# Issue order at the start of a one-core attention and two-FFN kernel, and scores one product later

## The chip, the cores and the metric

One core of a Trainium2 chip runs the whole program. The metric is the device time of one execution in microseconds (us), the median of several. TensorE (PE) does matrix products and transposes; ScalarE (ACT), VectorE (DVE) and GpSimd (POOL) work element by element; SyncE (SP) issues most transfers (DMA). Each engine works through its own queue of instructions in order, and semaphores hold an instruction until what it reads has been written and what it overwrites has been read. PSUM is the memory that TensorE writes; SBUF holds everything else.

## The reference

```python
B, H, S, Ns, D = 8, 8, 512, 32, 64
sc  = x @ state.T / sqrt(D);  a  = exp(sc  - max);  a  /= a.sum(-1)  + 1e-9;  xread = a  @ state
sc2 = state @ x.T / sqrt(D);  a2 = exp(sc2 - max);  a2 /= a2.sum(-1) + 1e-9;  sread = a2 @ x
y = concatenate([xread, sread], axis=2)      # per batch 544 tokens, 512 wide after the reshape
y = (silu(y @ w_gate) * (y @ w_val)) @ w_out                 # 512 -> 1536 -> 512
h = y @ w_in                                                 # 512 -> 2048
out = (maximum(h, 0) + alpha * minimum(h, 0)) @ w_out2       # 2048 -> 512
```

The weights arrive as float64, x and state as float32.

## The kernel before

**Products in parts.** Each operand of a large product is split into a high part, rounded for the fast fp32 mode of TensorE, and a low part (the rest), and each product is three passes: high by high, high by low, low by high (`PASSES`, line 19). A split is one ACT copy (`acopy`, line 77) and one DVE subtraction (`sub_lo`, line 83). The second pass needs the low part.

**Weights.** A `Unit` (line 243) turns 1 MB of float64 words into float32: a load (line 255), two passes on ACT (lines 264 and 265), and for each half two bit operations on DVE (lines 271 and 273) and an addition on POOL (line 278 into the tile `wr` of gate and value weights, line 281 otherwise). `Stream.step` (line 306) issues one half step: the ACT passes of one unit, the bits of the unit before it, the use of the one before that. `wr` number 0 needs units 0 and 1, number 1 units 2 and 3.

**Attention.** Of each of the 8 batches ("blocks"), heads go in two groups, u (g=0) and v (g=1). `xt` transposes x (blocks 0 and 1 on TensorE, line 151, with an ACT copy out of PSUM; the others on DVE); `scores` (line 159) are products with the state. For a first softmax, over the state's 32 entries, `first_cols`, `first_max`, `first_exp`, `first_scale` and `first_parts` work (the subtraction of the maximum at line 170 and the scaling at line 181 are on POOL; the result is transposed into `at` and split into `a`); for a second one, over the tokens, `second_max`, `second_exp`, `second_scale` (transposes, line 209) and `second_read` (line 219). The product of `a` with the state is folded into the first FFN: `state_times_w` (line 403) multiplies the state with `wr`, the result is split into `sw`, and gate and value are products of `sw` with `a` (`Block.product`, line 432).

**Stages.** First blocks 0 and 1 together, while weights still arrive: the list `order` (line 640) has 12 steps of gate, value, gate, value for one block and one weight tile; after the second gate of each step stands the `state_times_w` of the next. Their hidden values wait in SBUF. Then the projections of blocks 0 and 1 (`split`, `project`, line 462), with block 2's attention in between. Then blocks 2 to 7 one after the other in `ffn1` (line 473): for f = 0..11 a gate product, slot (f, 0), a value product, the split of the hidden values into `h`, slot (f, 1), the projection of the hidden values of f - 1, slot (f, 2). The slots carry the attention of the next block, `state_times_w` and conversions of the second FFN's weights (`stream2.step`, `one_later`; the tiles `sc` and `sp`). Last the second FFN (lines 769 and 823).

**What sets the order.** TensorE's instructions stand in the order in which the program calls them (`manual_schedule`, line 493). The other engines' queues are ordered by a scheduler that works with priorities by place in the program and with estimates; `tc.issue_after(x)` keeps what is inside behind x. PSUM has eight banks: acc0 to acc3, g, v and two `aux` in turn; an `aux` bank comes free when the last reader of it, often the DVE subtraction of an `sw` split, is done.

Of the kernel before, what the change touches and what calls it, by code (L numbers as in the profile page):

```python
# [8 lines left out]
F32 = mybir.dt.float32  # L9
# [3 lines left out]
AF = mybir.ActivationFunctionType  # L13
# [12 lines left out]
def attention_and_two_ffns(ctx: ExitStack, tc: tile.TileContext, x, state, w_gate, w_val,  # L26
# [60 lines left out]
    nc.vector.memset(warm, 0.0)  # L87
    nc.scalar.activation(warm, warm, AF.Exp)
    ident = const.tile([P, P], F32, tag="ident", name="ident")
# [11 lines left out]

    stt, xq, xn, wraw, wo1, sw, a1, srs = {}, {}, {}, {}, {}, {}, {}, []

    def load_state(b, eng=nc.sync):
        t = sm.tile([P, H, Ns], F32, tag="st", name=name("st"), bufs=1)
        for hp in range(2):
            for e in range(2):
                q = 64 * hp + 32 * e
                eng.dma_start(t[q:q + 32], state[b, :, :, 32 * e:32 * e + 32].rearrange("h n d -> n h d"))
        for hp in range(2):  # L110
            q = slice(64 * hp, 64 * hp + 64)
            for jj in range(2):
                h = 4 * jj + 2 * hp
                nc.vector.transpose(out=bd[b % 2][q, jj, :, Ns * hp:Ns * hp + Ns], in_=t[q, h:h + 2])
        stt[b] = sm.tile([P, H, Ns], F32, tag="stt", name=name("stt"), bufs=2)
        nc.vector.transpose(out=stt[b].rearrange("p h n -> p (h n)"), in_=t.rearrange("p h n -> p (h n)"))
# [11 lines left out]
    def load_xn(b, g):  # L128
        src = x[b].rearrange("(h g) (p c) d -> g p h c d", g=NG, c=SC)[g]
        if b < XT:  # L130
            t = t4([P, SC, 4, D], F32, "xn")
            for h in range(4):
                (nc.scalar if b == 0 and g and h % 2 else nc.sync).dma_start(t[:, :, h], src[:, h])
        else:
# [5 lines left out]
    class Attention:  # L140
# [42 lines left out]
        def first_parts(self, lo=True):  # L183
            b, g = self.b, self.g
            self.at = t2([P, S], F32, "at")
            nc.vector.transpose(out=self.at, in_=self.s1.rearrange("p t n -> p (t n)"))
# [56 lines left out]
    class Unit:  # L243
# [23 lines left out]
        def bits(self, i):  # L267
# [4 lines left out]
                                    op1=ALU.logical_shift_left)  # L272
            nc.vector.scalar_tensor_tensor(out=m, in0=hi, scalar=-0x80000000, in1=t, op0=ALU.bitwise_and,  # L273
                                           op1=ALU.bitwise_or)
            if self.place:
# [143 lines left out]
    class Block:  # L419
# [27 lines left out]
        def value(self, f):  # L447
            nc.vector.tensor_tensor(out=self.p[f], in0=self.p[f], in1=self.product(f, 1, "v"), op=ALU.mult)  # L448

# [43 lines left out]
    with tc.manual_schedule(engines={mybir.EngineType.PE}):  # L493
        load_state(0, nc.scalar)
        for g in range(NG):
            load_xn(0, g)
        stream1.load(2)
        for g in range(NG):
            load_xn(1, g)
        load_state(1)  # L500
        stream1.load(4)
        nc.sync.dma_start(alpha_sb, alpha.rearrange("(k p) -> p k", p=P))
        u, v = att[0, 0], att[0, 1]
        w, z = units1[0], units1[1]
# [16 lines left out]
        w.bits(0)  # L521
        v.second_max()
        v.first_exp()
# [5 lines left out]
        z.bits(0)  # L529
        z.bits(1)  # L530
        q.product()
        u.second_exp()
        p.product()
        q.parts()
        v.second_exp()
        v.first_parts()
        p.parts()
        stream1.skip(2)
        stream1.step(4)
# [17 lines left out]
        def ffn1_slots(b):  # L557
# [20 lines left out]
            if b + 1 < B:  # L578
# [5 lines left out]
                for f, th in attention(nb, (2, 3, 5, 6, 6), 4):  # L584
                    put(f, 0, th)
                put(NF1 - 2, 2, lambda: state_times_w(nb, 0))
# [39 lines left out]
        def raise_all():  # L626
            with tc.issue_after(gates[1].ins):
                for t in (u, v):
                    t.first_exp()
                    t.second_exp()  # L630

        extra = {0: [[lambda: u.xt(0), lambda: u.xt(1), u.scores, u.first_cols],
                     [lambda: v.xt(0), lambda: v.xt(1), u.first_max, u.second_max],
                     [v.scores, v.first_cols, v.first_max, v.second_max], [raise_all, u.first_scale]],
                 1: [[v.first_scale], [u.first_parts], [v.first_parts], []],
# [4 lines left out]
        order = [(0, 0), (0, 1), (1, 0), (1, 1)] + [(b, j) for j in range(2, NJ1) for b in range(XT)]  # L640
        gates = []
        for n, (b, j) in enumerate(order):
            for i in range(4):
                f = 2 * j + i // 2
                if i % 2:
                    blocks[b].value(f)
                elif n == 1 and i == 0:
                    with tc.issue_after(v.raised2.ins):
                        gates.append(blocks[b].gate(f))
                else:  # L650
                    gates.append(blocks[b].gate(f))
                for th in extra.get(n, ((),) * 4)[i]:
                    th()
                if i % 2:
                    stream1.step()
                if i == 2 and n + 1 < len(order):
                    nb, nj = order[n + 1]
                    stream1.until(2 * nj + 1, 1)
                    state_times_w(nb, nj)
        stream1.until(2 * NJ1 + EARLY - 1, 1)  # L660
# [16 lines left out]
        for b in range(XT):  # L677
            for f in range(NF1):
                with tc.issue_after(gates[-3 if f < 2 and not b else -1].ins):
                    blocks[b].split(f)  # L680
                if b == 0:
                    stream1.until(2 * NJ1 + f // 2, 2)
                if f or b:
# [264 lines left out]
```

## Time and profile before

| what | value |
|---|---|
| median of 3 runs | 1445.13 us (1442.11 to 1447.69) |
| the profiled execution's own time | 1446.67 us |
| its span in the profile | 1444.9 us |
| mean granted TensorE clock | 0.986 |
| TensorE busy | 1396.0 us, 97% |
| VectorE, ScalarE, GpSimd busy | 955.5, 516.0, 172.7 us |

The span runs from the first to the last instruction that the profiler recorded; 1.8 us of the execution's own time lie around it. TensorE works almost without a break, so the profile is read by where TensorE stands idle and which engine releases it, and by the clock that it was granted.

### The profile page before, as it was taken

How to read it: one execution, taken by the hardware profiler on the slowest of the kernel's cores; microseconds unless marked ns; L12 is line 12 of the kernel's file. 1: busy time of each engine (PE TensorE's matmuls, PEld its weight loads, DVE VectorE, ACT ScalarE, POOL GpSimd, SP SyncE). 2: the span in 40 equal slices, each digit the busy share in tenths (PEclk: the TensorE clock that was granted, in tenths of full speed). 3: DMA queues.
4: the chain of work that ended last, by engine and by line, in shares of the span. 5: the costliest groups of instructions: out<-in, count | busy, mean ns of one | idle time of the engine just before them, and what ended most of it. 6: DMA issues, size and time to landing. Idle time of an engine off the chain costs nothing.

```text
span 1444.9 us, 18973 instructions
## 1 busy us (share of the span) xinstructions
PE 1396.0 (97%) x7352; PEld 1094.0 (76%) x7352; DVE 955.5 (66%) x1606; ACT 516.0 (36%) x822; POOL 172.7 (12%) x150
## 2 busy tenths in 40 slices
PE   3899999999999999999999999999999999999997
PEld 1566877766767776777988888888888888888886
DVE  5686746778687776434746668676867668666653
ACT  4766335555464644434522112211222112211111
POOL 3351211324232332000000000000000000000000
PEclk6899999999999999999999999999999999999999
DMA  9443314364556443010546324742375324733465
GB/s 255 160 126 93 89 32 121 119 204 161 186 160 202 138 142 121 27 34 11 202 182 218 114 77 182 264 170 91 132 254 221 114 88 182 260 118 124 146 218 205
DMA packets 141586, 214.64 MB, mean 149 GB/s; under 512 B 78008, under 2 KB 85176, under 8 KB 136376
## 3 DMA queue, kind: packets, MB, share of 16 engines
q1 hardware_dynamic: 139352, 213.03, 44.0%
q8 instruction: 58, 0.95, 0.3%
q10 hardware_dynamic: 2144, 0.39, 0.1%
q14 instruction: 32, 0.26, 0.1%
HBM read 169.88 MB, written 43.52 MB: 148 GB/s over the span
## 4 chain that ended last, share of the span: by engine, by line
PE 85%; DVE 5%; ACT 4%; DMA 3%; issue 2%; POOL 0%; ACTq 0%; SPq 0%; DVEq 0%; POOLq 0%
PE acc L462 16%; PE acc L823 14%; PE aux L823 12%; PE v L769 9%; PE v L432 9%; PE g L432 8%; PE aux L769 6%; PE g L769 6%; PE aux L403 3%; DMA xn<-in_x_dram 2%; PE v L873 1%; PE g L873 1%; ACT h L77 1%; ACT raw L264 1%; DVE sw L83 1%
## 5 line engine op out<-in xcount | busy, mean ns | idle before, releaser
L462 PE MATMUL acc<-h,wp 128*128 128x512 f32 (+1 forms) x1296 | 294.9, 378 | 0.0
L462 PEld LDWEIGHTS acc<-h,wp 128*128 128x128 f32 x1296 | 233.4, 188 | 48.7 <-issue 2.5
L77 ACT ACTIVATE h<-m 128x512 fp32r<-128x512 f32 (+1 forms) x144 | 87.6, 609 | 448.3 <-DVE m L754 448.3
L823 PE MATMUL acc<-wo,h 128*128 128x512 f32 x864 | 219.9, 390 | 2.0 <-ACT h L77 1.7
L823 PE MATMUL aux<-wo,h 128*128 128x512 f32 x768 | 194.9, 389 | 0.0
L823 PEld LDWEIGHTS acc<-wo,h 128*128 128x128 f32 x864 | 161.1, 188 | 35.5 <-ACT h L77 2.1
L775 DVE TENSOR_TENSOR u<-v,p 128x512 f32<-128x512 f32 x96 | 66.2, 690 | 168.4 <-PE v L769 167.8
L823 PEld LDWEIGHTS aux<-wo,h 128*128 128x128 f32 x768 | 144.2, 188 | 29.9
L432 PE MATMUL g<-a,sw 128*128 128x512 f32 x576 | 154.2, 403 | 4.6 <-ACT sw L77 3.4
L432 PE MATMUL v<-a,sw 128*128 128x512 f32 x576 | 153.9, 403 | 1.2 <-DVE m L273 0.9
L432 PEld LDWEIGHTS g<-a,sw 128*128 128x128 f32 x576 | 105.6, 190 | 59.1 <-issue 20.1
L769 PE MATMUL v<-x,w 128*128 128x512 f32 x576 | 146.2, 389 | 0.0
L432 PEld LDWEIGHTS v<-a,sw 128*128 128x128 f32 x576 | 105.1, 189 | 42.8 <-issue 14.8
L769 PEld LDWEIGHTS v<-x,w 128*128 128x128 f32 x576 | 108.1, 188 | 22.4
L83 DVE TENSOR_TENSOR h<-m,h 128x512 fp32r<-128x512 f32 (+1 forms) x144 | 94.7, 658 | 16.1 <-ACT h L77 12.8
L448 DVE TENSOR_TENSOR s<-s,v 128x512 f32<-128x512 f32 (+1 forms) x84 | 54.1, 644 | 76.2 <-PE v L432 66.1
L769 PE MATMUL g<-x,w 128*128 128x512 f32 x384 | 97.6, 389 | 0.0
L769 PE MATMUL aux<-x,w 128*128 128x512 f32 x384 | 97.4, 389 | 0.0
L83 DVE TENSOR_TENSOR sw<-aux,sw 128x512 fp32r<-128x512 f32 x96 | 62.6, 681 | 52.3 <-ACT sw L77 52.1
L77 ACT ACTIVATE h<-s 128x512 fp32r<-128x512 f32 (+1 forms) x84 | 50.3, 599 | 98.1 <-DVE s L448 97.5
L281 POOL TENSOR_TENSOR m<-m,raw 128x512 int32<-128x512 int32 x44 | 62.8, 1429 | 183.6 <-DVE m L273 80.8
L769 PEld LDWEIGHTS aux<-x,w 128*128 128x128 f32 x384 | 72.1, 188 | 14.9
(120 smaller groups left out, 1606.9 us busy)
## 6 DMA issues: line engine op xcount, KB each, us to landing
w<-w2d SPq DMA_DIRECT2D x64, 896.0 KB, 6.2
wo<-wo2d SPq DMA_DIRECT2D x40, 1024.0 KB, 6.7
w2d<-sp SPq DMA_DIRECT2D x32, 512.0 KB, 2.7
raw<-in_moe_w_out_dram SPq DMA_DIRECT2D x14, 1024.0 KB, 5.3
out_dram<-o SPq DMA_DIRECT2D x34, 256.0 KB, 2.4
x2d<-xo SPq DMA_DIRECT2D x32, 256.0 KB, 2.5
raw<-in_moe_w_in_dram SPq DMA_DIRECT2D x8, 1024.0 KB, 8.1
wo2d<-sp SPq DMA_DIRECT2D x16, 512.0 KB, 3.6
```

The lines of the kernel that those rows point to most:

```text
L77: return nc.scalar.activation(o, i, AF.Copy)
L83: (eng or nc.vector).tensor_tensor(out=o, in0=src, in1=hi.bitcast(F32), op=ALU.subtract)
L264: nc.scalar.activation(hi.bitcast(F32), hi.bitcast(F32), AF.Copy, scale=REBIAS)
L281: nc.gpsimd.tensor_tensor(out=m, in0=m, in1=lo, op=ALU.add)
L403: nc.tensor.matmul(self.o[Ns * c:Ns * (c + 1), :], stt[b][q, 2 * c + g, :], wraw[j][q, c].rearrange("p k f -> p (k f)"), start=True, stop= ...
L432: nc.tensor.matmul(o[:, :self.n], self.lhs(f, k, a, which), self.rhs(k, c), start=(i == 0), stop=(i == last))
L448: nc.vector.tensor_tensor(out=self.p[f], in0=self.p[f], in1=self.product(f, 1, "v"), op=ALU.mult)
L462: nc.tensor.matmul(self.acc[e][:, :self.n], wo1[f // 2][:, f % 2, a, e * P:(e + 1) * P], t[:, c, :self.n], start=(f == 0 and i == 0), stop ...
L769: nc.tensor.matmul(o, w[a][:, q, c], x[k][:, q, e], start=start and n == 0, stop=stop and n == 5, skip_group_check=True)
L775: nc.vector.tensor_tensor(out=o, in0=x0, in1=x1, op=ALU.add)
L823: nc.tensor.matmul(o, h[:, c, a, u * P:(u + 1) * P], wos2[t][:, f, q], start=start and f == 0 and i == 0, stop=stop and f == 1 and i == 2)
L873: nc.tensor.matmul(o, w[a][:, k % 2, c], x[k // 2][:, k % 2, e, :NS], start=n == 0, stop=n == 11)
```

## The change

- Of block 0's x, group v, the parts h = 2 and 3 are now issued by ACT (before h = 1 and 3), and ACT issues them behind the first of its four state transfers and ahead of the other three. The first activation of the program (`warm`, with the load of its table) comes behind the last of them.
- Block 1's state is loaded from SP behind the raw weights of units 2 and 3 and the 8 KB of alpha; before it stood ahead of them.
- `at` of block 0 lies in the PSUM banks g and v.
- The 16 transposes of block 1's x stand ahead of the first `state_times_w` on TensorE; before they stood behind the first and second product. `second_max` and `second_exp` of v come later.
- In the two-block stage the steps of the weight stream are issued ahead of the step's attention work and are held behind the gate before last; the splits and the last conversions are held behind values too.
- In blocks 2 to 6 the scores of the next block (with what follows them in that stage) move from slot (f, 0) to slot (f, 1) for f = 3 and 7, which puts the value product ahead of them: ten places.

```diff
     nc.vector.memset(warm, 0.0)
-    nc.scalar.activation(warm, warm, AF.Exp)
...
     stt, xq, xn, wraw, wo1, sw, a1, srs = {}, {}, {}, {}, {}, {}, {}, []
+    issued = []
...
                 q = 64 * hp + 32 * e
-                eng.dma_start(t[q:q + 32], state[b, :, :, 32 * e:32 * e + 32].rearrange("h n d -> n h d"))
+                issued.append(eng.dma_start(
+                    t[q:q + 32], state[b, :, :, 32 * e:32 * e + 32].rearrange("h n d -> n h d")))
...
         if b < XT:
             t = t4([P, SC, 4, D], F32, "xn")
             for h in range(4):
-                (nc.scalar if b == 0 and g and h % 2 else nc.sync).dma_start(t[:, :, h], src[:, h])
+                (nc.scalar if b == 0 and g and h > 1 else nc.sync).dma_start(t[:, :, h], src[:, h])
         else:
...
         def first_parts(self, lo=True):
             b, g = self.b, self.g
-            self.at = t2([P, S], F32, "at")
+            self.at = psum([P, S], "v" if g else "g") if b == 0 else t2([P, S], F32, "at")
             nc.vector.transpose(out=self.at, in_=self.s1.rearrange("p t n -> p (t n)"))
...
-            nc.vector.scalar_tensor_tensor(out=m, in0=hi, scalar=-0x80000000, in1=t, op0=ALU.bitwise_and,
-                                           op1=ALU.bitwise_or)
+            self.made = nc.vector.scalar_tensor_tensor(
+                out=m, in0=hi, scalar=-0x80000000, in1=t, op0=ALU.bitwise_and, op1=ALU.bitwise_or)
...
         def value(self, f):
-            nc.vector.tensor_tensor(out=self.p[f], in0=self.p[f], in1=self.product(f, 1, "v"), op=ALU.mult)
+            return nc.vector.tensor_tensor(out=self.p[f], in0=self.p[f], in1=self.product(f, 1, "v"),
+                                           op=ALU.mult)
...
     with tc.manual_schedule(engines={mybir.EngineType.PE}):
-        load_state(0, nc.scalar)
         for g in range(NG):
             load_xn(0, g)
+        load_state(0, nc.scalar)
         stream1.load(2)
         for g in range(NG):
             load_xn(1, g)
-        load_state(1)
         stream1.load(4)
         nc.sync.dma_start(alpha_sb, alpha.rearrange("(k p) -> p k", p=P))
+        with tc.issue_after(issued[-1].ins):
+            nc.scalar.activation(warm, warm, AF.Exp)
         u, v = att[0, 0], att[0, 1]
         w, z = units1[0], units1[1]
         p, q = StateTimesW(0, 0, 0), StateTimesW(0, 0, 1)
             w.act()
         v.first_max()
         w.bits(0)
-        v.second_max()
...
         w.bits(1)
         with tc.issue_after(u.raised1.ins):
         u.first_parts()
         z.bits(0)
         z.bits(1)
+        for t in (att[1, 0], att[1, 1]):
+            t.xt(0)
+            t.xt(1)
         q.product()
         u.second_exp()
         p.product()
         q.parts()
-        v.second_exp()
         v.first_parts()
         p.parts()
+        v.second_max()
+        v.second_exp()
+        load_state(1)
         stream1.skip(2)
...
                 for f, th in attention(nb, (2, 3, 5, 6, 6), 4):
-                    put(f, 0, th)
...
-        extra = {0: [[lambda: u.xt(0), lambda: u.xt(1), u.scores, u.first_cols],
-                     [lambda: v.xt(0), lambda: v.xt(1), u.first_max, u.second_max],
-                     [v.scores, v.first_cols, v.first_max, v.second_max], [raise_all, u.first_scale]],
+        def columns(t):
+            t.scores()
+            with tc.issue_after(units1[3].made.ins):
+                t.first_cols()
+
+        extra = {0: [[lambda: columns(u)], [lambda: columns(v), u.first_max, u.second_max],
+                     [v.first_max, v.second_max], [raise_all, u.first_scale]],
...
-        gates = []
...
                 if i % 2:
-                    blocks[b].value(f)
+                    values.append(blocks[b].value(f))
...
                     gates.append(blocks[b].gate(f))
+                with tc.issue_after(gates[max(0, len(gates) - 2)].ins):
+                    if n == i == 0:
+                        stream1.until(3, 1)
+                    if i % 2:
+                        stream1.step()
+                    if i == 2 and n + 1 < len(order):
+                        stream1.until(2 * order[n + 1][1] + 1, 1)
                 for th in extra.get(n, ((),) * 4)[i]:
                     th()
-                if i % 2:
-                    stream1.step()
                 if i == 2 and n + 1 < len(order):
-                    nb, nj = order[n + 1]
-                    stream1.until(2 * nj + 1, 1)
-                    state_times_w(nb, nj)
+                    state_times_w(*order[n + 1])
...
-                with tc.issue_after(gates[-3 if f < 2 and not b else -1].ins):
+                k = -3 if f < 2 and not b else -1
+                with tc.issue_after(gates[k].ins), tc.issue_after(values[k].ins):
                     blocks[b].split(f)
                 if b == 0:
-                    stream1.until(2 * NJ1 + f // 2, 2)
+                    with tc.issue_after(values[-1].ins):
+                        stream1.until(2 * NJ1 + f // 2, 2)
```

POOL at the start of the program, from u's scaling on; `s_18`/`s_16` are u's softmax tile, `s_25`/`s_23` v's, `s_65`/`s_74` block 1's, `wr` weight tiles, `raw_137`/`raw_136` unit 0, `raw_140`/`raw_139` unit 1, `raw_164`/`raw_152` and `raw_167`/`raw_155` units 2 and 3. Before:

```order
L181 TENSOR_TENSOR s_18_188<-s_18_188,r_27_216 128x512
L181 TENSOR_TENSOR s_25_210<-s_25_210,r_35_243 128x512
L278 TENSOR_TENSOR wr_230<-m_29_226,raw_137 128x2x256
L278 TENSOR_TENSOR wr_230<-m_33_236,raw_137 128x2x256
L278 TENSOR_TENSOR wr_230<-m_38_253,raw_140 128x2x256
L278 TENSOR_TENSOR wr_230<-m_40_258,raw_140 128x2x256
L278 TENSOR_TENSOR wr_305<-m_53_301,raw_164 128x2x256
L278 TENSOR_TENSOR wr_305<-m_56_307,raw_164 128x2x256
L170 TENSOR_TENSOR s_65_338<-s_65_338,m_71_362 128x512
L278 TENSOR_TENSOR wr_305<-m_74_373,raw_167 128x2x256
```

and now:

```order
L182 TENSOR_TENSOR s_16_177<-s_16_177,r_25_205 128x512
L279 TENSOR_TENSOR wr_219<-m_27_215,raw_136 128x2x256
L279 TENSOR_TENSOR wr_219<-m_30_222,raw_136 128x2x256
L182 TENSOR_TENSOR s_23_199<-s_23_199,r_32_229 128x512
L279 TENSOR_TENSOR wr_219<-m_35_239,raw_139 128x2x256
L279 TENSOR_TENSOR wr_219<-m_37_244,raw_139 128x2x256
L279 TENSOR_TENSOR wr_333<-m_61_329,raw_152 128x2x256
L279 TENSOR_TENSOR wr_333<-m_64_335,raw_152 128x2x256
L279 TENSOR_TENSOR wr_333<-m_69_354,raw_155 128x2x256
L279 TENSOR_TENSOR wr_333<-m_71_359,raw_155 128x2x256
L171 TENSOR_TENSOR s_74_367<-s_74_367,m_82_393 128x512
```

The first two conversions moved ahead of v's scaling, and those of units 2 and 3 ahead of the subtractions of block 1 (line 170 before, 171 now).

ACT near the end of the two-block stage, ahead of the split of the `sw` that belongs to the last weight tile and block 0 (`sw_1100` before, `sw_1112` now). Before:

```order
L445 ACTIVATE p_1070<-g_1092 128x512
L265 ACTIVATE raw_1061<-raw_1061 128x1024
L77 ACTIVATE sw_1100<-aux_1101 128x512
L77 ACTIVATE sw_1100<-aux_1106 128x512
L77 ACTIVATE wp_1132<-m_214_1065 128x512
```

and now:

```order
L446 ACTIVATE p_1075<-g_1104 128x512
L265 ACTIVATE raw_968<-raw_968 128x1024
L266 ACTIVATE raw_968<-raw_968 128x1024
L265 ACTIVATE raw_1092<-raw_1092 128x1024
L77 ACTIVATE sw_1112<-aux_1113 128x512
L77 ACTIVATE sw_1112<-aux_1118 128x512
L266 ACTIVATE raw_1092<-raw_1092 128x1024
```

Where one conversion pass stood between the second gate's activation and the split, three stand now.

DVE in block 3, from the value of f = 4 on; `h_2845` is the hidden tile of that f, `v_2837` and `v_2911` the value products of f = 4 and 5, `sw_2868` the next step's split, `e2t_2909` the copy of the transposes. Before (the seven rows that follow are alike in both):

```order
L448 TENSOR_TENSOR s_2816<-s_2816,v_2837 128x512
L83 TENSOR_TENSOR h_2845<-s_2816,h_2845 128x512
L83 TENSOR_TENSOR sw_2868<-aux_2869,sw_2868 128x512
L83 TENSOR_TENSOR sw_2868<-aux_2874,sw_2868 128x512
L271 TENSOR_SCALAR m_527_2852<-raw_2479 128x512
```

and now:

```order
L449 TENSOR_TENSOR s_2816<-s_2816,v_2837 128x512
L83 TENSOR_TENSOR sw_2868<-aux_2869,sw_2868 128x512
L83 TENSOR_TENSOR sw_2868<-aux_2874,sw_2868 128x512
L272 TENSOR_SCALAR m_527_2852<-raw_2479 128x512
L352 TENSOR_TENSOR sc_2883<-m_456_2483,m_465_2539 128x128
L274 SCALAR_TENSOR_TENSOR m_527_2852<-raw_2479,m_527_2852 128x512
L352 TENSOR_TENSOR sc_2883<-sc_2883,m_456_2483 128x128
L352 TENSOR_TENSOR sc_2883<-m_456_2483 128x128
L352 TENSOR_TENSOR sc_2883<-m_465_2539,sc_2883 128x128
L80 COPY e2t_2909<-aux_2904 128x512
L449 TENSOR_TENSOR s_2888<-s_2888,v_2911 128x512
L83 TENSOR_TENSOR h_2845<-s_2816,h_2845 128x512
```

The subtraction that makes the low part of `h_2845` moved from the second row to the last, behind the value of f = 5. On TensorE the projection of `h_2845` stands right behind `v_2911` in both. The same is found in blocks 4 and 5 at the same f (`h_3615`, `h_4385`) and at no other of the ten places.

## Rows read from the trace of the kernel before

**Rows 1.** The page, part 1: busy time and share of the span, TensorE.
```profile
PE 1396.0 (97%) x7352; PEld 1094.0 (76%) x7352; DVE 955.5 (66%) x1606; ACT 516.0 (36%) x822; POOL 172.7 (12%) x150
```

**Rows 2.** Windows: busy us by engine, then granted clock, DMA share, GB/s.
```profile
0.00:20.00 20.00, 7.97 (x24) 3.87 (x24) 5.65 (x17) 7.43 (x10) 1.75 (x7) 0.79 0.86 220
20.00:36.00 16.00, 4.43 (x17) 0.90 (x18) 15.67 (x35) 9.06 (x14) 10.56 (x9) 0.50 0.94 298
36.00:60.00 24.00, 19.88 (x80) 11.80 (x79) 14.59 (x30) 18.43 (x26) 9.27 (x9) 0.79 0.68 242
60.00:140.00 80.00, 76.79 (x555) 50.66 (x554) 60.14 (x109) 52.62 (x77) 26.60 (x21) 1.00 0.29 87
```

**Rows 3.** Waits of TensorE, 0 to 250 us: total, times, longest.
```profile
PE aux L403 <- POOL wr L278: 14.8, 3, 10.3
PE aux L151 <- DMA xn<-in_x_dram: 9.3, 2, 5.1
PE g L432 <- ACT sw L77: 3.4, 3, 2.2
...
PE v L432 <- DVE m L273: 0.9, 1, 0.9
PE g L432 <- DVE sw L83: 0.8, 2, 0.5
PE g L432 <- ACT p L445: 0.4, 1, 0.4
```

**Rows 4.** Timeline of TensorE, first 57 us: start, length, engine, line; idle before.
```profile
7.27 1.95 PE L159 MATMUL acc<-xt,bd 128*64 128x512 f32 x4
13.43 1.94 PE L151 MATMUL aux<-ident,xn 128*128 128x128 f32 x8 [4.20 <-DMA xn<-in_x_dram]
...
31.31 1.95 PE L403 MATMUL aux<-wr,stt 64*32 64x512 f32 x12 [1.04 <-POOL wr L278]
35.44 3.07 PE L432 MATMUL g<-a,sw 128*128 128x512 f32 x6 [2.18 <-ACT sw L77]
38.31 1.39 PE L151 MATMUL aux<-ident,xn 128*128 128x128 f32 x8
...
42.99 1.04 PE L151 MATMUL aux<-ident,xn 128*128 128x128 f32 x8
...
50.80 1.95 PE L403 MATMUL aux<-wr,stt 64*32 64x512 f32 x12 [3.40 <-POOL wr L278]
52.67 2.93 PE L432 MATMUL v<-a,sw 128*128 128x512 f32 x6
```

**Rows 5.** Timeline of GpSimd, first 52 us.
```profile
25.77 5.48 POOL L278 TENSOR_TENSOR wr<-m,raw 128x512 int32<-128x512 int32 x4
...
49.46 1.28 POOL L278 TENSOR_TENSOR wr<-m,raw 128x512 int32<-128x512 int32 x1
```

**Rows 6.** Timeline of TensorE near the end of the two-block stage.
```profile
132.25 0.73 PE L432 MATMUL g<-a,sw 128*128 128x512 f32 x2 [0.69 <-ACT sw L77]
```

**Rows 7.** Waits of TensorE, 160 us to the end.
```profile
PE aux L159 <- DVE sw L83: 6.5, 7, 1.0
```

**Rows 8.** Timeline of TensorE, 302 to 326 us, in block 3.
```profile
308.07 1.08 PE L159 MATMUL aux<-xt,bd 128*64 128x512 f32 x4 [0.97 <-DVE sw L83]
...
321.87 1.64 PE L432 MATMUL v<-a,sw 128*128 128x512 f32 x6
323.35 2.89 PE L462 MATMUL acc<-h,wp 128*128 128x512 f32 x12
```

**Rows 9.** Timeline of VectorE, the same stretch.
```profile
319.07 0.69 DVE L83 TENSOR_TENSOR h<-s,h 128x512 fp32r<-128x512 f32 x1 [0.86 <-ACT h L77]
320.62 0.69 DVE L83 TENSOR_TENSOR sw<-aux,sw 128x512 fp32r<-128x512 f32 x1 [0.86 <-ACT sw L77]
...
325.60 0.68 DVE L80 COPY e2t<-aux 128x512 f32<-128x512 f32 x1
```

**Rows 10.** Timeline of ScalarE, the same stretch: one conversion pass.
```profile
320.48 1.14 ACT L264 ACTIVATE raw<-raw 128x1024 f32<-128x1024 f32 x1
```

More of the change, by code (lines that the diff above doesn't have):

```diff
@@ L584, in ffn1_slots @@
                 for f, th in attention(nb, (2, 3, 5, 6, 6), 4):
-                    put(f, 0, th)
+                    put(f, 1 if f in (3, 7) else 0, th)
                 put(NF1 - 2, 2, lambda: state_times_w(nb, 0))
@@ L640, in attention_and_two_ffns @@
         order = [(0, 0), (0, 1), (1, 0), (1, 1)] + [(b, j) for j in range(2, NJ1) for b in range(XT)]
-        gates = []
+        gates, values = [], []
         for n, (b, j) in enumerate(order):
```

## The prediction

> **What bounds the kernel now.** I read the page's busy times first: TensorE is busy 97% [rows 1], so an edit can only win where TensorE stands idle or runs at half clock, and it loses wherever it makes TensorE wait. The windows show where that is: 7.97 of the first 20 us and 4.43 of the next 16 are busy, at a granted clock of 0.79 and 0.50; from 36 to 60 us 19.88 of 24 at 0.79; from 60 to 140 us 76.79 of 80 at full clock [rows 2]. TensorE's waits name the releasers: 14.8 us for POOL's conversions into `wr` (three times), 9.3 us for x (twice), and 3.4 + 0.9 + 0.8 + 0.4 = 5.5 us before gate and value products [rows 3]. After 160 us one wait matters: 6.5 us, seven times, before scores, released by the DVE subtraction that frees their `aux` bank [rows 7]. The timeline then gives each place.
>
> **The start, step by step.** In the timeline u's scores begin at 7.27, v's transposes only at 13.43, after 4.20 us of waiting for x; the first state products end at 33.26 (31.31 + 1.95), held by a train of four conversions, 25.77 to 31.25; the first gate product follows at 35.44, 4.2 us after the train [rows 4, 5].
>
> ACT now issues v's two parts of x ahead of three state transfers. That is 256 KB in front of the state, at the 220 GB/s of the first 20 us [rows 2] an estimated 1.2 us for u's scores: they end near 7.27 + 1.2 + 1.95 = 10.4, and v's transposes start there, 3.0 us sooner. (Bounds: nothing sooner, if the bytes in front keep x as late as now; 4.2 us at most, the wait itself.)
>
> POOL's first two conversions now pass v's scaling. Their bits are made by DVE before 24 us already, so POOL no longer stands idle ahead of its train; with v's operations 3.0 us sooner and four conversions of 5.48 / 4 = 1.37 us, I take the train's end at 26.2, 5.0 us sooner. Behind it the same 4.2 us of state products and splits, and 0.9 us for ACT copies of block 1's transposes, which now stand in ACT's queue there: first gate product 26.2 + 4.2 + 0.9 = 31.3, **4.1 us gained** (bounds 0 and 5.0).
>
> Behind it three things leave TensorE's path. The 16 transposes of block 1 (1.39 + 1.04 us [rows 4]) move into the wait for the train: **2.4**. The wait for the next `wr` (3.40 before 50.80 [rows 4]): the last conversion ended at 49.46 + 1.28 = 50.74 [rows 5], because block 1's subtractions, which wait for scores, stood ahead of it on POOL; now four stand in a row behind the first train, 26.2 + 4 x 1.37 = 31.7 at the soonest, and with the ACT passes and bits that they need near 37. The fourth product needs them at about 40, so the **3.4** goes. What is late next is the split of that step's `sw`, whose length is the same in both. The `at` of block 0 in PSUM, the later state of block 1 and v's later second maximum I cost at nothing: block 1's scores stand behind the first product, and v's second exponential is wanted by transposes two steps later. If that cover is gone, the scores are as late as the state, about a microsecond. Sum by here: 4.1 + 2.4 + 3.4 = 9.9.
>
> The clock: after the 3.40 us wait twelve state matmuls took 1.95 us and the value product 2.93 [rows 4], a granted half clock; the same value product takes 1.64 at full clock [rows 8]. [...] From the rows one value product at half clock costs 2.93 - 1.64 = 1.3 us; I count none, and let 2 us either way go into the range.
>
> **Later in that stage it loses.** ACT's order puts three conversion passes ahead of the split of the last `sw` of block 0, and two passes, two `h` copies and a weight copy ahead of block 1's. A pass is 1.14 us [rows 10]. Behind the last gate's activation (0.6) come three passes (3.4) and the copy of the split (0.6): 4.6 us, against 1.1 of state products and 1.5 of value product on TensorE, so it waits 2.0. For the other: 0.6 + 2.3 + 1.2 + 0.6 + 0.6 = 5.3 against 2.6, so 2.7. Now 0.69 + 0.51 is waited at such a place (the 0.69 is in [rows 6]; the 0.51 is the longer of the two waits for a subtraction, 0.5, in [rows 3]). **Loss 4.7 - 1.2 = 3.5** (bounds 0, if the passes slip into idle time of ACT, and 6). The first stage as a whole: 9.9 - 3.5 = 6.4 gained.
>
> **Later blocks.** Scores now follow the value product (some 1.4 us from start to next start: 321.87 to 323.35 [rows 8]); the wait they had was never above 1.0 [rows 7], so all of the **6.5 us** goes. But at f = 3 of blocks 3, 4 and 5 the order on DVE moves the subtraction of the hidden tile behind the value of the next f. In the trace that subtraction ran at 319.07 [rows 9], four microseconds before its projection at 323.35 [rows 8]. Now DVE first does the two `sw` subtractions (the first at 320.62), bits and sums, the copy that starts at 325.60 [rows 9], the value and then the subtraction. ACT's conversion passes no longer stand between the two copies of `sw`, so I let this run start 0.6 us and end 1.5 us sooner: copy at 324.1, value 324.7, low part ready at 325.9. The value product ends near 322.4, a microsecond sooner than before, and the projection's first pass takes 0.2: it stands from 322.7 to 325.9, **3.2 us**. The transposes ahead wait 0.5 for their `aux` bank. Three places: **11.1 us lost** (bounds: 3.6, if only value and subtraction of 0.6 each follow the value product; 15, if DVE ends its run no sooner than now). Later blocks: 11.1 - 6.5 = 4.6 lost.
>
> **Sum.** -6.4 + 4.6 = -1.8 on the profiled execution's 1446.67 us, which lies 1.5 above the median; on the median of 1445.13 that is **1443.3 us**. 0.5% is 7.2 us, about what a measurement of this kernel can tell from no change.
>
> **Rivals.**
> 1. *The hidden tiles are not late.* The DVE run ends so much sooner that the lower bound holds: 3.6 lost for 6.5 gained. With the start's 6.4 that is -9.3, 1435.8; without the stalls near the end of the first stage 3.5 more, 1432.3. For it: ACT had idle time before the scores. Against: DVE's run between 320.62 and 325.60 is almost gapless [rows 9].
> 2. *x is no sooner.* The DMA engines are 0.86 and 0.94 busy in the first 36 us [rows 2], and the raw weights land as late as the bytes ahead of them. Then the train of conversions does not move; the transposes' 2.4 and the 3.4 stay, 3.5 are lost again, and 4.6 later: +2.3, 1447.4. [...]
> 3. *Conversions ahead of splits in every step (slower).* The steps of the weight stream are now issued ahead of the attention work in all 12 steps of the first stage. If ACT does as at the last two places in all eleven `sw` splits behind the first, at 2.0 us each, that is 22, of which 4.7 are in my sum: -1.8 + 17 = +15, 1460. It is slower than before from about 0.2 us more per split on. For it: the two places seen. Against: waits on splits in this stage are small now, 3.4 + 0.8 of which 2.18 is the first product's [rows 3, 4], and ACT is busy 52.62 of 80 us between 60 and 140 [rows 2].
>
> **How the numbers follow.** Forecast 0.48, rival 1 0.25, rival 2 0.12, rival 3 0.15. The forecast's own range, from its bounds, is 1436 to 1450: a twelfth of it is faster by over 7.2 us, a twentieth slower. Rival 1 is nearly all faster, rival 2 the same, two thirds of rival 3 slower by over 7.2 us, the rest the same. Faster 0.04 + 0.24 = 0.28, slower 0.02 + 0.10 = 0.12, same 0.60. The range 1432 to 1450 leaves out the far side of rival 3 and little else.
>
> **What would show it.** v's transposes near 10.4 us with no long wait for x; the first gate product near 31 us; no wait of 3 us before the second `wr`; waits of about 2 us at the last two `sw` splits; projections begin near 133 instead of 139.87; no waits before scores; three waits of about 3 us, released by the DVE subtraction of `h`, in blocks 3, 4 and 5. The prediction is wrong if the projections of blocks 3 to 5 don't wait, or if many small waits on `sw` appear between 60 and 130 us.

## The result, and the profile after

| | median us | lowest to highest | runs |
|---|---|---|---|
| before | 1444.16 | 1442.11 to 1447.69 | 4 |
| changed | 1465.07 | 1463.95 to 1469.50 | 4 |

The ratio is 1.0148, 95% interval 1.0118 to 1.0178: 20.9 us slower, where 1.8 us faster was forecast and the range ended at 1450. The profiled execution took 1465.55 us with a span of 1463.8 us; its mean granted clock is 0.980 (0.986 before), and TensorE was busy 1411.7 us instead of 1396.0 with the same 7352 matmuls. One execution of scores_back below, of 1570.36 us at a mean granted clock of 0.842 where the nine others had 0.988 to 0.993, is a slow one and is left out of its ratio.

The windows of the changed kernel (columns as in [rows 2]: length, busy us of PE, PEld, DVE, ACT, POOL, then the granted clock, DMA share, GB/s):

```profile
20.00:36.00 16.00, 11.17 (x44) 5.22 (x44) 15.16 (x37) 13.20 (x21) 9.93 (x8) 0.60 0.92 287
36.00:60.00 24.00, 20.48 (x166) 12.91 (x166) 21.45 (x44) 18.45 (x29) 12.36 (x11) 0.93 0.77 278
...
120.00:140.00 20.00, 16.68 (x69) 10.88 (x68) 14.20 (x24) 11.27 (x20) 3.91 (x3) 0.83 0.52 85
...
300.00:400.00 100.00, 94.72 (x526) 67.33 (x524) 70.26 (x129) 52.12 (x85) 30.75 (x26) 0.95 0.53 168
400.00:500.00 100.00, 90.72 (x515) 64.50 (x513) 69.12 (x128) 53.61 (x87) 28.59 (x24) 0.97 0.51 154
500.00:600.00 100.00, 97.95 (x581) 70.43 (x582) 69.63 (x124) 47.03 (x82) 29.20 (x25) 0.98 0.38 123
```

TensorE is better off at the start (11.17 us busy of 16, against 4.43; a clock of 0.93 from 36 to 60 us, against 0.79). But from 120 to 140 us (0.83) and in the three windows from 300 to 600 us (0.95, 0.97, 0.98) the clock is below the 1.00 that all four had before, and idle time grows. The middle one of the three windows of 300 to 600 us, before:

```profile
400.00:500.00 100.00, 97.27 (x591) 69.25 (x584) 77.61 (x140) 54.34 (x91) 31.66 (x27) 1.00 0.52 161
```

The waits of TensorE, 0 to 250 us, answer to [rows 3]:

```profile
PE aux L152 <- DMA xn<-in_x_dram: 7.8, 3, 5.2
PE g L433 <- ACT sw L77: 6.4, 4, 2.2
PE g L433 <- DVE sw L83: 3.2, 3, 1.6
...
PE aux L404 <- POOL wr L279: 2.0, 1, 2.0
```

The wait for `wr` shrank from 14.8 to 2.0 us, those on splits of `sw` grew from 3.4 + 0.8 to 6.4 + 3.2. From 160 us on, against the one row of [rows 7]:

```profile
PE acc L464 <- DVE h L83: 8.6, 3, 2.9
PE aux L210 <- DVE sw L83: 8.0, 6, 2.7
```

The 6.5 us before scores are gone, and 16.6 us stand in their place: three waits for the low part of `h`, six for the `aux` bank of the transposes. The timeline of TensorE shows the first stage's start and end (start, length, engine, line, operation; idle before and releaser):

```profile
11.18 1.69 PE L152 MATMUL aux<-ident,xn 128*128 128x128 f32 x8
...
24.65 3.23 PE L404 MATMUL aux<-wr,stt 64*32 64x512 f32 x16 [2.04 <-POOL wr L279]
30.03 2.93 PE L433 MATMUL g<-a,sw 128*128 128x512 f32 x6 [2.15 <-ACT sw L77]
...
43.42 2.07 PE L433 MATMUL g<-a,sw 128*128 128x512 f32 x4 [1.41 <-DVE sw L83]
...
53.58 1.20 PE L433 MATMUL g<-a,sw 128*128 128x512 f32 x4 [1.61 <-DVE sw L83]
...
117.61 1.92 PE L433 MATMUL g<-a,sw 128*128 128x512 f32 x6 [1.62 <-ACT sw L77]
...
121.76 1.63 PE L433 MATMUL g<-a,sw 128*128 128x512 f32 x6 [0.84 <-DVE m L274]
...
128.17 2.98 PE L433 MATMUL g<-a,sw 128*128 128x512 f32 x6 [2.16 <-ACT sw L77]
131.46 2.93 PE L433 MATMUL v<-a,sw 128*128 128x512 f32 x6 [0.32 <-DVE m L274]
134.19 2.10 PE L433 MATMUL g<-a,sw 128*128 128x512 f32 x6
...
137.49 12.86 PE L464 MATMUL acc<-h,wp 128*128 128x512 f32 x56
```

The first gate product is at 30.03 ([rows 4]: 35.44). Where 3.40 us were waited for the second `wr` before, three waits on splits stand now, 0.51 + 1.41 + 1.61 = 3.5 us between 41 and 54 us (0.55 + 0.28 at such places before). Then 1.62 + 0.84 + 2.16 + 0.32 us of waits near the end, and behind the wait of 2.16 products of 2.98, 2.93 and 2.10 us: the granted clock is 0.58 from 128.0 to 131.0 us and 0.50 from there to 135.2. From 60 to 115 us, at 1.00, such a product takes 1.5 to 1.8. Projections begin at 137.49, where 139.87 stood in the trace of before. In block 3, the place of [rows 8]:

```profile
318.55 0.75 PE L210 MATMUL aux<-ident,e 128*128 128x128 f32 x4 [0.49 <-DVE sw L83]
319.06 1.64 PE L433 MATMUL v<-a,sw 128*128 128x512 f32 x6
320.53 0.39 PE L464 MATMUL acc<-h,wp 128*128 128x512 f32 x1
323.78 5.06 PE L464 MATMUL acc<-h,wp 128*128 128x512 f32 x11 [2.86 <-DVE h L83]
328.64 2.13 PE L433 MATMUL g<-a,sw 128*128 128x512 f32 x6
```

and VectorE there ([rows 9]):

```profile
321.85 0.68 DVE L80 COPY e2t<-aux 128x512 f32<-128x512 f32 x1
322.45 0.67 DVE L449 TENSOR_TENSOR s<-s,v 128x512 f32<-128x512 f32 x1
323.04 1.47 DVE L83 TENSOR_TENSOR h<-s,h 128x512 fp32r<-128x512 f32 x2
```

The copy, the value and the two subtractions run without a gap; the projection's second pass waits 2.86 us for the first of these subtractions, and the eleven matmuls behind the wait take 5.06 us, the gate product 2.13: the granted clock is 0.51 from 323.8 to 330.0 us (twelve took 2.89 before, at 1.00 from 321.8 to 326.0). At f = 9 of blocks 3, 4 and 5 the transposes wait 1.93, 2.70 and 1.94 us. One row of each wait's place and the product behind it, blocks 3 and 5:

```profile
353.62 1.12 PE L210 MATMUL aux<-ident,e 128*128 128x128 f32 x4 [1.93 <-DVE sw L83]
354.39 2.91 PE L433 MATMUL v<-a,sw 128*128 128x512 f32 x6
```

```profile
528.71 0.75 PE L210 MATMUL aux<-ident,e 128*128 128x128 f32 x4 [1.94 <-DVE sw L83]
529.21 1.64 PE L433 MATMUL v<-a,sw 128*128 128x512 f32 x6
```

Behind nearly the same wait the value product takes 2.91 us once, at a granted clock of 0.50 (354.4 to 357.1 us), and 1.64 once, at 1.00 (529.2 to 530.7). What makes the transposes wait there begins on ScalarE, here in block 4:

```profile
429.97 1.14 ACT L265 ACTIVATE raw<-raw 128x1024 f32<-128x1024 f32 x1 [1.30 <-DMA raw<-in_moe_w_out_dram]
431.01 1.11 ACT L266 ACTIVATE raw<-raw 128x1024 int32<-128x1024 uint32 x1
432.14 1.28 ACT L202 ACT_TABLE_LOAD   x1
...
436.05 0.60 ACT L446 ACTIVATE s<-g 128x512 f32<-128x512 f32 x1
438.66 0.63 ACT L77 ACTIVATE h<-s 128x512 fp32r<-128x512 f32 x1 [2.02 <-DVE s L449]
439.20 1.07 ACT L77 ACTIVATE sw<-aux 128x512 fp32r<-128x512 f32 x2
```

Two conversion passes are ahead of the table load for the exponentials now; that load begins 5.5 us behind the scores (at 426.62), where it began 3.1 us behind them before (TensorE's row and ScalarE's, block 4 before):

```profile
416.49 1.08 PE L159 MATMUL aux<-xt,bd 128*64 128x512 f32 x4 [0.87 <-DVE sw L83]
...
419.62 1.28 ACT L201 ACT_TABLE_LOAD   x1 [3.14 <-issue]
```

So the activation of f = 8 comes at 436.05, 4.0 us after its gate product ended (430.49 + 1.52), the value and the `h` copy follow, and the split of `sw`, whose subtraction frees the `aux` bank, is pushed to 439.20. VectorE adds to it: when that activation ends, at 436.65, the last of four sums and a row sum stand ahead of the value on VectorE, which starts 1.3 us later (VectorE's row, then TensorE's):

```profile
437.95 0.67 DVE L449 TENSOR_TENSOR s<-s,v 128x512 f32<-128x512 f32 x1
...
441.39 0.75 PE L210 MATMUL aux<-ident,e 128*128 128x128 f32 x4 [2.70 <-DVE sw L83]
```

### The profile page after: what moved, and what is told of

Read it like the earlier page. It is cut to its first block, busy times and chain, and to the rows that moved or that the text cites. A ratio compares the mean times of both kernels' runs of the same rounds, so it can differ in the third digit from the quotient of the medians.

```text
span 1463.8 us, 19000 instructions
## 1 busy us (share of the span) xinstructions
PE 1411.7 (96%) x7352; PEld 1102.7 (75%) x7352; DVE 950.2 (65%) x1606; ACT 517.0 (35%) x822; POOL 175.1 (12%) x150
## 4 chain that ended last, share of the span: by engine, by line
PE 87%; DVE 5%; ACT 3%; DMA 2%; issue 2%; POOL 0%; SPq 0%; ACTq 0%; DVEq 0%; POOLq 0%
PE acc L464 17%; PE acc L839 13%; PE aux L839 12%; PE g L433 9%; PE v L433 9%; PE v L785 9%; PE aux L785 6%; PE g L785 6%; PE aux L404 3%; DMA raw<-in_moe_w_out_dram 1%; ACT raw L265 1%; PE v L889 1%; PE g L889 1%; DVE sw L83 1%; DVE h L83 1%
## 5 line engine op out<-in xcount | busy, mean ns | idle before, releaser
L464 PE MATMUL acc<-h,wp 128*128 128x512 f32 (+1 forms) x1296 | 302.9, 385 | 8.6 <-DVE h L83 8.6
L464 PEld LDWEIGHTS acc<-h,wp 128*128 128x128 f32 x1296 | 237.3, 192 | 66.9 <-issue 10.6
L433 PE MATMUL g<-a,sw 128*128 128x512 f32 x576 | 159.1, 410 | 10.5 <-ACT sw L77 6.4
```

Source lines behind the costliest of these rows:

```text
L433: nc.tensor.matmul(o[:, :self.n], self.lhs(f, k, a, which), self.rhs(k, c), start=(i == 0), stop=(i == last))
L464: nc.tensor.matmul(self.acc[e][:, :self.n], wo1[f // 2][:, f % 2, a, e * P:(e + 1) * P], t[:, c, :self.n], start=(f == 0 and i == 0), stop ...
```

## Experiments

Times are medians in us; "before" was run beside each (1444.3 to 1445.1), and the ratio is to it.

**scores_back** undoes the scores' move in the changed kernel:

```diff
-                    put(f, 1 if f in (3, 7) else 0, th)
+                    put(f, 0, th)
```

> The changed kernel with one thing undone: the scores of the later blocks stand ahead of the value product again, as before the change. Theory (the scores' move makes the whole loss: 16.6 us of new waits in blocks 2 to 6 in place of 6.5, and the half clock behind them): the later blocks cost what they cost before, and what stays is the first stage, whose projections began 2.4 us sooner (137.49 against 139.87), so 1444 - 2.4 = about 1442 us. Rival (the rest of the change shifts conversions into the later blocks and these make the waits): the three waits on the subtraction of h and the waits of the transposes stay, about 1463 us.

1447.23, ratio 1.0014 (1.0002 to 1.0026): 17.8 us of the 20.9 go. In the trace of the same kernel run again (scores_back_2 below) the later waits before scores are 6.5 us, as before.

**scores_only** makes the same move in the kernel before.

> The kernel before with the scores' move alone (ten places in blocks 2 to 6). Theory: three waits near 2.9 us on the subtraction of h, waits of the transposes near 8 us in all, a clock near 0.95 to 0.98 between 300 and 600 us, and 1444 + 23 = about 1467 us. Rival (the move by itself only takes away the 6.5 us of waits before scores): about 1438 us.

1460.78, ratio 1.0104 (1.0087 to 1.0121), 16 us slower. The theory's waits are there and its clock too (0.96 to 0.99 between 300 and 600 us); its 1467 was 6 us too high. The waits from 160 us on:

```profile
PE aux L209 <- DVE sw L83: 8.1, 7, 3.0
PE acc L462 <- DVE h L83: 7.5, 3, 2.9
```

In its trace the start, which is that of before, is itself quicker than in the trace that the prediction read: v's transposes begin at 11.44 and the projections at 137.81.

```profile
11.44 1.94 PE L151 MATMUL aux<-ident,xn 128*128 128x128 f32 x8 [1.36 <-DMA xn<-in_x_dram]
...
33.44 3.08 PE L432 MATMUL g<-a,sw 128*128 128x512 f32 x6 [2.17 <-ACT sw L77]
```

**h_ahead** holds, in the changed kernel, what slot (f, 2) issues behind the split of `h`:

```diff
...
-            fill(f, 2)
+            with tc.issue_after(blk.parts[0].ins), tc.issue_after(blk.parts[1].ins):
+                fill(f, 2)
```

> The changed kernel, with what slot (f, 2) issues on ScalarE and VectorE held behind the two halves of the hidden tile's split of the same f, so that the low part of h is made ahead of the splits of sw. Theory (the place of that subtraction in VectorE's queue costs three waits of 2.9 us and the half clock behind each, some 2 to 3 us): 1465 - 8.6 - 7, and 2 us more for the transposes, whose aux bank comes free later: about 1451 us. Rival (VectorE and ScalarE are simply full there, and the wait changes its name): the transposes or the next products wait as long, 1462 to 1467 us.

1447.29, ratio 1.0012 (1.0003 to 1.0022): 17.8 us gained, more than the theory's 14. The waits for `h` are gone, those of the transposes stay at 7.8 us but none is longer than 1.6, and the granted clock is 1.00 from 300 to 600 us (the first two of the three windows):

```profile
PE aux L210 <- DVE sw L83: 7.8, 6, 1.6
```

```profile
300.00:400.00 100.00, 97.54 (x570) 69.49 (x569) 71.62 (x139) 58.46 (x93) 30.57 (x27) 1.00 0.59 183
400.00:500.00 100.00, 95.35 (x579) 68.32 (x577) 71.31 (x137) 53.51 (x90) 31.22 (x28) 1.00 0.53 167
```

TensorE is busy 1402.0 us here and 1411.7 in the changed kernel, and idle 43.6 and 52.1 (span less busy). So of the 18.2 us between the two spans 8.5 are idle time and 9.7 are matmuls that ran slower. In block 3 the two conversion passes still stand ahead of the table load, which begins 4.9 us behind the scores (4.8 in the changed kernel). But VectorE now does the sums behind the value, and the transposes at f = 9 wait 0.85 us instead of 1.93:

```profile
349.67 0.75 PE L210 MATMUL aux<-ident,e 128*128 128x128 f32 x4 [0.85 <-DVE sw L83]
```

So the passes alone do not make that wait; how much of it is ScalarE's and how much VectorE's stays open.

**wait_filled** leaves the waits and fills them: 12 matmuls whose results nobody uses, ahead of the projection that waits for `h`.

```diff
+            if f == 5 and blk in blocks[3:6]:
+                o = psum([P, S], "g")
+                for _ in range(12):
+                    nc.tensor.matmul(o, blk.lhs(f, 0, 0, 0), blk.rhs(0, 0), start=True, stop=True)
```

> The changed kernel with 12 added matmuls (512 columns, into the bank g, results unused) ahead of the projection at f = 5 in blocks 3, 4 and 5, where TensorE stands idle for 2.9 us until the low part of h is there: 12 x 0.23 = 2.8 us of work in the wait's place. Theory (half of what these three waits cost is the clock that falls behind them): the work costs nothing, the clock stays at full, the first matmuls behind it take their usual time (2.9 us for twelve instead of 5.1), and the time falls by 6 to 9 us, to 1456 to 1459 us, although TensorE has more to do. Rival (the clock falls for another cause, or costs little there, and the wait is all of it): 1465 us or, with the added work behind the wait, up to 1473.

1455.05 in the profiled run, 1460.83 to 1462.03 in three others; ratio 1.0104 (1.0080 to 1.0129). In the profiled run the theory holds: the work in the wait's place adds no time (1465.55 in the changed kernel's profiled run), the twelve matmuls behind it take 2.88 us in block 3 and 3.31 in block 4, and the granted clock is 1.00 in all three windows from 300 to 600 us.

```profile
320.94 2.89 PE L490 MATMUL g<-a,sw 128*128 128x512 f32 x12
323.67 2.88 PE L464 MATMUL acc<-h,wp 128*128 128x512 f32 x12
```

Why three runs stayed 6 us higher, that trace could not say; in it the value product takes 1.64 us behind all three waits at f = 9 (0.97, 2.12 and 1.99 us). **all_filled** puts 8 more such matmuls ahead of the transposes at f = 9 in the same blocks.

> wait_filled, and 8 more added matmuls (into the bank v, results unused) ahead of the transposes at f = 9 in blocks 3, 4 and 5, where the changed kernel waits 1.9, 2.7 and 1.9 us. Theory (a wait of about 2 us lowers the clock in some executions and not in others; in the changed kernel's trace it fell behind two of these three): all executions now lie at 1452 to 1456 us, none near 1461. Rival (the 1461 us have another cause): a median near 1461 us again, or above by the added work.

1457.87 (1456.35 to 1460.23), ratio 1.0095 (1.0075 to 1.0115). The median is 2 us above the band of the theory, and 3.2 us below wait_filled's with 5.5 us more work, though the intervals of the two ratios overlap; the granted clock is 1.00 in all three windows from 300 to 600 us (the first of them):

```profile
300.00:400.00 100.00, 99.07 (x564) 71.36 (x563) 73.21 (x135) 55.07 (x90) 30.63 (x26) 1.00 0.56 178
```

With 20 matmuls more in each of three blocks it is 7.2 us faster than the changed kernel. The intervals of these two ratios do not overlap. So with these waits filled the clock is back (1.00 against 0.95 to 0.98 between 300 and 600 us), and the gain is of the size of the 9.7 us that h_ahead's busy time shows. That the clock at f = 9 makes the spread of wait_filled's runs is not shown.

**steps_back** is scores_back with the weight stream's steps behind the attention work again, in all 12 steps of the first stage; `first_cols` of block 1 is no longer held behind a unit's bits either.

> As scores_back, and the steps of the weight stream in the first stage stand behind the attention work again and are not held behind gates, as before the change. The start (x, state, transposes, maxima, at in PSUM) stays as changed. Theory (conversions ahead of the splits of sw cost 8.3 us of waits and half clock at the last two steps of that stage against 2.1 before, and buy little, since block 1's scores come early anyway by now): first gate product near 30 us as in the changed kernel, projections begin near 132 to 134 us, 1437 to 1439 us. Rival (the conversions in front are what brings the second wr early): a wait of 3 us before the second wr returns, projections begin near 137, 1442 us or more.

1441.74, ratio 0.9974 (0.9964 to 0.9985): 5.5 us faster than scores_back, between the two expectations and next to the rival's 1442. Waits of 1.54 and 2.44 us before the second `wr` come back, as the rival says, and yet the projections begin at 135.94. The largest wait of the stage's end is now before its last value product:

```profile
133.27 2.88 PE L433 MATMUL v<-a,sw 128*128 128x512 f32 x6 [2.00 <-DVE m L274]
```

**scores_back_2** is scores_back again, for its trace.

> scores_back once more, for an undisturbed trace. Theory (the new first stage ends where the old one ends: what the start wins, 3 to 6 us, goes in waits of 1.6 to 2.2 us and half clock at the stage's last two steps): projections begin between 137 and 139 us, as in the traces of the kernel before (139.9) and of scores_only (137.8); later blocks as before. Rival (something in the later blocks costs the 2 us): the later waits before scores are longer than 6.5 us.

One run, 1446.8. Projections begin at 138.40, the later waits before scores are 6.5 us: the theory's side.

**x_only** has the transfers' order alone, on the kernel before.

> The kernel before with the new order of transfers at the start alone: v's two parts of x on ScalarE ahead of three state transfers, the first activation behind them (block 1's state stays where it was). Theory (as first written: v's transposes waited for x until 13.43, so they come up to 3 us sooner, and with them the conversions): 3 us faster, about 1442 us. Rival (in another profile with the old order those transposes began at 11.44, so the 13.43 was one execution's; and the conversions wait for GpSimd's order, not for x): no change, 1444 to 1446 us, the first gate product at 33 to 35 us.

1445.41, ratio 1.0002 (0.9992 to 1.0012): the rival. **tr_only** moves the 16 transposes alone.

> The kernel before with the 16 transposes of block 1 moved ahead of the first state products, and nothing else. Theory (they move into TensorE's wait for the conversions): 2.4 us faster, about 1442 us. Rival (the copies of these transposes stand in ScalarE's queue ahead of the conversions, and the first product comes later by what is saved behind it): no change, 1444 to 1446 us.

1442.39, ratio 0.9986 (0.9974 to 0.9998): 2.7 us by the medians, 2.0 by the ratio, on the theory's side.

**steps_first2** keeps the steps in front in the first two of 12 steps only.

> As scores_back, but the steps of the weight stream are issued ahead of the attention work and held behind gates only in the first two of the 12 steps of the first stage; from the third step on they stand behind it as before the change. Theory (in front they win where the second wr is waited for, 4 us at 40 to 44 us in steps_back, and lose near the end of the stage): the waits on splits of sw near 115 to 130 us shrink from 1.6 + 2.2 us to about 1 each, projections begin near 132 us, about 1439 us. Rival (what is won early is lost again at the next wait, since the stage's end is set by the raw weights of w_out): projections near 136, 1441 to 1444 us.

1441.20, ratio 0.9979 (0.9970 to 0.9988). Projections begin at 133.87; still 1.20, 1.19 and 0.97 us are waited near the end. The time lies in the rival's band, 1441 to 1444; the waits on splits near the end, 0.69 and 1.20, are the theory's.

**banks_free** is steps_back with

```diff
-                    banks=("acc0", "acc1") if j < EARLY else ("g", "v"))
+                    banks=("acc0", "acc1") if j < EARLY else None)
```

> As steps_back, and the bit operations of the weight units from w_out number 2 on no longer use the PSUM banks g and v for their first result, so that the last products of the first stage need not wait for them. Theory (the wait of 2.00 us before the last value product and the half clock behind it, 2.88 against 1.65, are set by these banks): 3 us faster than steps_back, about 1438.5 us. [...]

1437.88, ratio 0.9955 (0.9941 to 0.9970): the theory. The wait of 2.00 us is gone, and the last value product takes 1.52 us instead of 2.88; projections begin at 129.51. **both** adds steps_first2.

> banks_free and steps_first2 together: free banks for the last conversions, and the weight stream's steps in front in the first two steps only. Theory (they act at different places, the second wr and the end of the stage): waits before the second wr gone, no wait before the last value product, about 1437 us. Rival (the stage's end is bound by the last splits of sw and the hidden tiles on ScalarE): as banks_free, 1438 to 1440 us.

1438.52, ratio 0.9960 (0.9946 to 0.9975): no more than banks_free. Its trace waits 5.7 us on the subtractions of splits, where banks_free's waits 3.4 us for `wr` and 1.3 on such a subtraction. **sums_behind** is banks_free, with the sums and splits that keep the scores' `aux` bank busy held behind the last subtraction of an `sw` split (`last_split`):

```diff
...
+            with tc.issue_after(last_split[0].ins):
+                later.pop(0)()
...
```

> banks_free, and what the second FFN's weights still need in later blocks (the sums sc, their parts sp) is held on VectorE behind the last subtraction of an sw split. Theory (the 6.5 us of waits before the later blocks' scores come from four sums of some 2 us that stand ahead of the sw subtractions on VectorE, so the order there frees the aux bank, and the scores need not move): the seven waits before scores go, 1438 - 6.5 = about 1431.5 us. Rival (the sums then delay the maxima and the exponentials, and a wait of the transposes or of h takes their place): 1437 us or more.

1436.14 (1434.42 to 1437.57), ratio 0.9940 (0.9922 to 0.9957): faster than both kernels, by 8.5 us and by 28.9. But of the 6.5 us expected only some 2 came over banks_free, and the intervals of the two overlap; of the waits before scores 2.6 us are left, and 1.4 us of waits on VectorE's copies out of the projections' banks are new:

```profile
PE aux L160 <- DVE sw L83: 2.6, 3, 0.9
...
PE acc L467 <- DVE xo L80: 1.4, 4, 0.3
```

**both_sums** is sums_behind with the steps of steps_first2.

> sums_behind with the steps of the weight stream in front in the first two steps (as in both). Theory: what both and sums_behind win adds up, about 1430 us. Rival: the one hides the other, no better than sums_behind.

1437.18, ratio 0.9955 (0.9939 to 0.9972): the rival, nothing added.

## Why the prediction was wrong, point by point

- **Later blocks: the step that failed.** It forecast 4.6 us lost; scores_back shows 17.8, scores_only 16. The three places and their size were right: 3 x 3.2 us for `h` against 8.6 measured, 0.5 for the transposes ahead against 0.49 to 0.50, and the 6.5 us before scores did go. Two terms were missing. First, the waits at f = 9 of the same blocks, 1.9 + 2.7 + 1.9 = 6.5 us: the prediction looked for subtractions of `h` that had moved in VectorE's queue, and took the other seven places as free, without following what comes behind the scores there, the exponentials on ScalarE and the value on VectorE, to the next split of `sw`. Second, the clock: behind five of the six waits of 1.93 to 2.86 us TensorE ran at a lower clock for a stretch, the longest at 0.51 from 323.8 to 330.0 us; that is 9.7 us in all by the busy times of this trace and h_ahead's. The trace of before had shown that price (3.40 us of waiting, then 1.95 and 2.93 us [rows 4]), and the prediction worked it out for the start and put it at nothing; at the new waits it was not asked for. Against scores_back_2, whose span is 1445.0 with 1401.4 busy, idle time grew by 8.5 and busy time by 10.3: 18.8 us, half of it clock.
- **The end of the first stage.** Forecast 3.5 us lost. Waits went from 0.69 + 0.51 + 0.94 = 2.1 to 4.9, and half clock behind them adds 2.98 + 2.93 + 2.10 less 3 x 1.55 = 3.4: 6.2 us. The order on ScalarE was read rightly (2.0 and 2.7 us forecast before the two splits, 1.62 and 2.16 measured), and again it was the clock that was left out. (steps_back: 5.5 us back.)
- **The start.** The first product was forecast at 31.3 and came at 30.03. But the comparison was with one execution in which x came late. In traces with the old transfers v's transposes begin at 10.09 to 13.43 (tr_only, before), and x_only is no faster: the term for x was nothing, and that 31.3 came out near is in part luck. Against scores_only's start, with x at 11.44 where the changed kernel has it at 11.18, the first product is still 3.4 us sooner (33.44 to 30.03); that is left to the other orders at the start, and no run has GpSimd's alone. The transposes' 2.4 us held (tr_only 2.0 to 2.7). The wait for the second `wr` went, as forecast, but its 3.4 us did not stay won: the split behind it, which the prediction took to be the same in both, and the next one are waited for, 3.5 us against 0.8.
- **First stage as a whole.** Forecast 6.4 us gained; scores_back is 2 us slower than before (1.0014), so that all of it was lost again, and the projections begin at 138.4 instead of 137.8 to 139.9.
- **Rivals.** The slower one, conversions ahead of splits in every step of the first stage, did not come: the waits on splits are 9.6 us in all, of which 2.15 are the first product's, 3.5 lie between 41 and 54 us, 3.8 at the last two steps and 0.15 between 60 and 115 us. 1460 for it is near the result by chance, since the loss lies elsewhere. "x is no sooner" was right about x. "The hidden tiles are not late" fell with the three waits for `h`.
- **The clock.** Between 300 and 600 us the granted clock is 1.00 in the kernel before, 0.95 to 0.98 in the changed one and 1.00 in h_ahead. The 1.95 and 2.93 us behind the wait of 3.40 [rows 4] spoke against the longer ones of the new waits, and a lower clock there should have been a rival: in the changed kernel's trace the clock fell behind five of the six between 1.93 and 2.86 us (to 0.50 to 0.58, each over the 2.0 to 6.2 us that follow), and behind none of the three of 0.5 (1.00 in the 1.4 us that follow each).

## What to carry to other kernels

Price a new wait on TensorE twice: its idle time, and the stretch at a lower clock that may stand behind it; here the nine new waits, 0.5 to 2.9 us long, added 8.5 us of idle time over the kernels without them and 9.7 to 10.3 us of slower matmuls. When one instruction is moved a product later, follow the whole chain behind it on the other engines to the next release of the buffers that TensorE needs, not only the queue that visibly changed. If a wait is for a bank, first see what stands ahead of the instruction that frees it: putting the sums behind it cut the waits from 6.5 to 2.6 us, where moving the scores made 16.6 of them; that it wins time over banks_free, some 2 us, is not clear of noise.

## What was unexpected of the hardware

- A wait of about 2 us was followed by a lower clock in one place and not in another: 1.93 us in block 3 by a value product of 2.91 us at a granted clock of 0.50, 1.94 us in block 5 by one of 1.64 us at 1.00.
- Useless matmuls in a wait made the kernel faster: 36 more matmuls, 4.0 us off the median (1465.07 to 1461.12) and 10.5 off the profiled run; 60 more, 7.2 off the median. For the 60 the intervals of the ratios lie apart (1.0118 to 1.0178 without, 1.0075 to 1.0115 with); for the 36 they overlap.
- With the same order of transfers, TensorE began on v's x anywhere between 10.09 and 13.43 us; one trace of the start is not enough to price a transfer.
